# Six tiles of their own for the transposed probabilities, scale products four at a time, and new engine orders

## The chip, the core and the metric

The kernel runs on one core of a Trainium2 chip. The core has five engines that each work through their own list of instructions in order: TensorE (PE, matrix products), VectorE (DVE), ScalarE (ACT), GpSimd (POOL) and SyncE (SP), which in this kernel issues the DMA transfers. The metric is the time of one execution on the device in microseconds, as the median of several runs.

## What is computed

Attention over pooled queries, then a bilinear feed-forward layer. The inputs `q`, `k`, `v` are 4 batches x 8 heads x 1152 positions x 64.

```python
def _attn_ref(q, k, v):
    B, H, S, D = q.shape
    factor = 2
    scale = 1.0 / np.sqrt(D)
    q_pool = q.reshape(B, H, S // factor, factor, D).mean(axis=3)
    scores = scale * np.matmul(q_pool, k.transpose(0, 1, 3, 2))
    scores = scores - np.max(scores, axis=-1, keepdims=True)
    attn = np.exp(scores)
    attn = attn / (np.sum(attn, axis=-1, keepdims=True) + 1e-09)
    return np.matmul(attn, v).astype(np.float32)

def _moe_ref(x, w_a, w_b, w_out):
    a = x @ w_a
    b = x @ w_b
    return (a * b @ w_out).astype(np.float32)
```

`x` is the attention's output with the heads side by side: 2304 tokens x 512. `w_a` and `w_b` are 512 x 1536, `w_out` is 1536 x 512.

## The kernel before, in words

**Staging.** Work on a batch goes by pairs of heads, in passes: a pass takes some query rows of one pair, in blocks of 128 rows of one head. Batch 0 has eight passes, two rounds over its four pairs. For each block PE makes the scores (L682, from batch 2 on L685 with operands split into two f16 parts), DVE copies them with a bound on the row's maximum (L717, `sm_max`), ACT takes the exponential (L724), and DVE makes the factor of the row from its sum (L728, L734). What follows depends on the pass:
- In the first four passes (`N_PE = 4`) PE transposes the f32 block in pieces of up to 4 x 128 columns into PSUM (L760, `tr_pe`), ACT or DVE copies each piece into the tile `pt` (L771 or L773, `tr_out`, by the letters of `EVICT`), and PE multiplies it by `v` (L804, `pv_f`). The row factors go through a diagonal matrix (L776, `r_diag`; L780, `r_wide`; L784, `r_mul`).
- In all later passes ACT and DVE write the scaled block as two f16 parts, high and low, into one of three buffers `p` (L737, L741), SP issues one DMA transpose of it into `pt` (L747, `transpose`), and PE multiplies by the two f16 parts of `v` (L838, `pv`).

ACT moves the product out of PSUM (L848, `x_copy`), and ACT, POOL and DVE split and scale it into the f16 parts `xt` (L871, L875, L881). Beside the first four passes run the weights, 12 slices f of 128 columns: loaded by SP (L552), rebuilt from 64-bit numbers by ACT, POOL and DVE (L558, L577, L581, L588), their magnitude taken on ACT or DVE (L567, L570) and summed over the partitions on PE (L597, `w_sum`). DVE makes a scale of each sum (L600, `w_scale`; L605), and ACT and DVE or POOL split each slice into two parts (L622; L626, L631, L635). Then comes the feed-forward layer by tiles of 256 tokens: PE multiplies `xt` by the weights of `a` and `b` (L919, `moe_mm`, 24 products for each f of a tile), ACT and DVE form `g` from them with the scales in `cc` (L926, L931), ACT and POOL split `g` (L936, L939), and PE multiplies by `w_out` (L945).

**The tile of transposed probabilities.** `pt` is one tile in SBUF, `[128, 2, NCH, NR * 128]` in f16: two parts, nine chunks of 128 positions, and `NR = 6` slots of 128 columns. Each block has the slot of its number modulo 6. The early passes see the same bytes as f32, in the view `ptf`, and use two slots' columns of it for two heads. Waits between instructions that touch one tile are drawn by the framework from the regions that they touch.

**Scales.** `w_cc` (L609) multiplies the two scales of one f by the scale of batch 0 into `cc`, two instructions of one element in each partition; it is called once for each of the 12 f. For batches 1 to 3 one instruction does all f at once (L519).

**What sets the order.** Everything above is a task of the class `Plan`: an engine, a duration, a key, a function and the names that it reads and writes. The five rows of the table `ORDERS` (PE, DVE, ACT, POOL, SP) list the numbers of the tasks in the order in which each engine gets them. `Plan.order` merges the five into one program order; the instructions of one engine then run strictly in that order.

Of the kernel before, what the change touches and what calls it, by code (L numbers as in the profile page):

```python
# [7 lines left out]
F32 = mybir.dt.float32  # L8
# [20 lines left out]
REMN = 64  # L29
N_PE, EVICT = 4, "ADADA"  # L30
# [180 lines left out]
    ),  # L211
)

# [964 lines left out]
```

## Time and profile before

| | |
|---|---|
| median of 3 runs | 839.35 us (837.95 to 842.45) |
| profiled execution | 840.88 us, span in the trace 839.1 us |
| mean granted clock of TensorE | 0.981 of full speed |
| PE busy | 781.5 us (93%) |
| DVE busy | 619.8 us (74%) |
| ACT busy | 580.0 us (69%) |
| POOL busy | 242.4 us (29%) |
| instructions in the trace | 21333 |

The profile records one execution. The span runs from the first instruction to the last; the execution's own time is 1.8 us longer. An engine is busy while it carries out an instruction, not while it waits for a semaphore. Where the profile names a releaser for an idle time, it is the instruction or transfer whose end came last before the idle engine went on.

### The profile page before, as it was taken

The numbers are of one execution on the slowest core, as the hardware profiler recorded it, in microseconds if no ns is written. First come the engines' busy times: TensorE is split into PE (matmuls) and PEld (weight loads), VectorE is DVE, ScalarE is ACT, GpSimd is POOL, SyncE is SP. The second block draws the span as 40 slices with busy tenths as digits, with TensorE's granted clock in tenths as the row PEclk, the third lists the DMA queues.
The fourth block names the chain that finished last, engine by engine and source line by source line (L and its number), as shares of the span: only waits on it lengthen the run. The fifth ranks groups of instructions, "written<-read, shape, count | busy, mean of one in ns | idle before, by whom it ended". The sixth has DMA issues, their size and how long they took to land.

```text
span 839.1 us, 21333 instructions
## 1 busy us (share of the span) xinstructions
PE 781.5 (93%) x8864; PEld 603.4 (72%) x8864; DVE 619.8 (74%) x1215; ACT 580.0 (69%) x986; POOL 242.4 (29%) x226
## 2 busy tenths in 40 slices
PE   6877458989999998999999999999999999999998
PEld 3654336767677776787777877887788788887886
DVE  4998878978998898999999999889687634032110
ACT  4999897878778787788888789777666643233222
POOL 5668674323310222201132104101301221301203
PEclk9998969999999999999999999999999999999999
DMA  7655748899999999999999999899867616000100
GB/s 262 208 188 204 208 144 192 211 199 196 209 212 210 195 200 189 232 173 217 192 185 211 182 206 194 164 171 173 151 127 127 127 30 128 13 26 1 27 2 25
DMA packets 316289, 132.32 MB, mean 158 GB/s; under 512 B 300832, under 2 KB 302880, under 8 KB 316192
## 3 DMA queue, kind: packets, MB, share of 16 engines
q1 hardware_dynamic: 316192, 130.96, 75.1%
q8 instruction: 69, 1.13, 0.5%
q14 instruction: 28, 0.23, 0.1%
HBM read 50.72 MB, written 4.72 MB: 66 GB/s over the span
## 4 chain that ended last, share of the span: by engine, by line
PE 57%; DVE 2%; DMA 1%; ACT 0%; issue 0%
PE ab L919 26%; PE ab L945 15%; PE sps L685 8%; PE xps L838 8%; DMA pt<-p 1%; DVE p L741 1%; DVE s L717 1%; PE sps L682 0%; DVE g L931 0%; ACT g L926 0%; DVE o L951 0%; PE xps L496 0%; ACT p L737 0%; ACT s L724 0%; PE xps L429 0%
## 5 line engine op out<-in xcount | busy, mean ns | idle before, releaser
L919 PEld LDWEIGHTS <-wab 128*128 128x128 f16 x2592 | 252.2, 99 | 37.3 <-issue 6.3
L919 PE MATMUL ab<-xt,wab 128*128 128x256 f16 x2304 | 262.7, 274 | 2.7 <-DVE xt L881 0.9
L724 ACT ACTIVATE s<-s,st 128x1152 f32<-128x1152 f32 x144 | 179.9, 1250 | 34.5 <-DVE s L717 34.0
L939 POOL TENSOR_TENSOR gl<-g,gh 128x256 fp32r<-128x256 f32 x108 | 94.5, 880 | 358.1 <-ACT gh L936 349.7
L741 DVE SCALAR_TENSOR_TENSOR p<-s,st,p 128x1152 f16<-128x1152 f32 x128 | 181.5, 1424 | 10.0 <-ACT p L737 9.5
L737 ACT ACTIVATE p<-s,st 128x1152 f16<-128x1152 f32 x128 | 159.0, 1248 | 37.9 <-DMA pt<-p 13.3
L945 PE MATMUL ab<-wo,gh 128*128 128x512 f32 x432 | 139.8, 405 | 1.7 <-DVE g L931 1.7
L682 PE MATMUL sps<-k,q 64*128 64x512 f32 (+3 forms) x448 | 103.9, 557 | 22.6 <-DVE s L717 10.5
L926 ACT ACTIVATE g<-ab,cc 128x256 f32<-128x256 f32 (+1 forms) x144 | 55.4, 415 | 90.4 <-PE ab L919 90.3
L717 DVE TENSOR_SCALAR_CACHE_REDUCE s<-sps 128x1152 f32<-128x1152 f32 x72 | 96.7, 1350 | 25.7 <-PE sps L682 24.5
L717 DVE TENSOR_SCALAR_CACHE_REDUCE s<-sps,ksc 128x1152 f32<-128x1152 f32 x72 | 101.0, 1410 | 15.7 <-PE sps L685 15.3
L838 PE MATMUL xps<-pt,vs 128*64 128x128 f16 (+1 forms) x3888 | 109.3, 215 | 1.4 <-DMA pt<-p 1.1
L838 PEld LDWEIGHTS <-vs 128*64 128x64 f16 x3888 | 100.5, 110 | 13.5 <-issue 11.6
L931 DVE SCALAR_TENSOR_TENSOR g<-ab,cc,g 128x256 f32<-128x256 f32 (+1 forms) x144 | 55.2, 410 | 72.6 <-ACT g L926 72.6
L682 PEld LDWEIGHTS sps<-k,q 64*128 64x128 f32 (+1 forms) x448 | 48.5, 187 | 75.4 <-issue 52.4
L945 PEld LDWEIGHTS ab<-wo,gh 128*128 128x128 f32 x432 | 77.9, 188 | 20.4 <-ACT g L926 1.7
L945 PE MATMUL ab<-wo,gl 128*128 128x512 f32 x216 | 85.4, 395 | 0.0
L936 ACT ACTIVATE gh<-g 128x256 fp32r<-128x256 f32 x108 | 43.8, 411 | 54.8 <-PE ab L945 54.1
L685 PE MATMUL sps<-k,q 64*128 64x512 f16 (+3 forms) x624 | 65.5, 341 | 0.0
L685 PEld LDWEIGHTS <-q 64*128 64x128 f16 (+1 forms) x720 | 36.2, 97 | 39.6 <-issue 7.0
L581 POOL TENSOR_SCALAR xt<-xt 128x512 f16<-128x512 f32 x22 | 51.9, 2357 | 35.3 <-ACT xt L577 25.9
L419 POOL TENSOR_TENSOR q<-qraw 128x576 f32<-128x576 f32 (+2 forms) x20 | 25.0, 1250 | 92.3 <-PE sps L682 48.9
(120 smaller groups left out, 737.1 us busy)
## 6 DMA issues: line engine op xcount, KB each, us to landing
k<-in_k_dram SPq DMA_DIRECT2D x19, 576.0 KB, 4.7
vraw<-in_v_dram SPq DMA_DIRECT2D x17, 576.0 KB, 4.9
xt<-in_w_ab_dram SPq DMA_DIRECT2D x15, 512.0 KB, 3.6
qraw<-in_q_dram SPq DMA_DIRECT2D x12, 576.0 KB, 4.5
out_dram<-o SPq DMA_DIRECT2D x16, 256.0 KB, 3.8
xt<-in_w_out_dram SPq DMA_DIRECT2D x7, 512.0 KB, 3.3
g<-in_w_ab_dram SPq DMA_DIRECT2D x5, 512.0 KB, 4.2
wab<-in_w_ab_dram SPq DMA_DIRECT2D x4, 512.0 KB, 3.5
```

Of the source, the lines that this page charges most:

```text
L682: nc.tensor.matmul(out, q, k, start=True, stop=True)
L685: nc.tensor.matmul(out, q[:, hq], k[:, hk], start=(hq, hk) == (0, 0), stop=(hq, hk) == (1, 0))
L717: nc.vector.tensor_scalar(out=s_t[sbuf(i)], in0=sps[:, at:at + S], scalar1=-1.0 / 16.0 if u is None else ksc[:, u, 4:5], scalar2=None, op0 ...
L724: nc.scalar.activation(out=s, in_=s, func=AF.Exp, scale=-1.0, bias=t[:, 0:1], accum_out=t[:, 1:2])
L737: nc.scalar.activation(out=p_t[pbuf(i)][:, 0], in_=s_t[sbuf(i)], func=AF.Copy, scale=st_t[i % NST][:, 3:4])
L741: nc.vector.scalar_tensor_tensor(out=p[:, 1], in0=s, scalar=st_t[i % NST][:, 3:4], in1=p[:, 0], op0=ALU.mult, op1=ALU.subtract)
L838: nc.tensor.matmul(xps[half(e), at:at + w], vs[:, c, e, hv], pt[:, hp, c, c0:c0 + w], start=(c == 0 and n == 0), stop=(c == NCH - 1 and n ...
L919: nc.tensor.matmul(dst if t < 8 else dst.rearrange("p (b n) -> p b n", b=B), wab[:, f, 1 - m, a, c], moe_x(t, b, c), start=(n == 0), stop= ...
L926: nc.scalar.activation(out=g_t[:, f, c], in_=ab[j][:, 1, c], func=AF.Copy, scale=cc[:, b, f, 0:1])
L931: nc.vector.scalar_tensor_tensor(out=g, in0=ab[j][:, 0, c], scalar=cc[:, b, f, 1:2], in1=g, op0=ALU.mult, op1=ALU.mult)
L939: nc.gpsimd.tensor_tensor(out=gl_t[j], in0=g_t[:, f], in1=gh_t[j].bitcast(F32), op=ALU.subtract)
L945: nc.tensor.matmul(acc[u], g[:, us], wo[:, f, a], start=(first and n == 0), stop=(last and n == 2))
```

## The change

`pt` becomes a list of six tiles, one for each slot, each `[128, 2, NCH, 128]`; `ptf` becomes a list of f32 views of them. In the early passes a head's block now lies in the tile of its own slot. `w_cc` makes the scales of four f (`CC_F = 4`) in one instruction with eight elements in each partition: three instructions in place of 24. Since this changes the number of tasks and their numbering, every row of `ORDERS` is new, and the order is another one. In DVE's order before, L609 stands 12 times ahead of the first L881 that frees an L919 product; in the new order it stands there twice. Before, nine of PE's sums L597 stand ahead of the first L919, now ten.

```diff
@@ -27,6 +27,7 @@
 P_SCALE = 2.0 ** 14
 
 REMN = 64
+CC_F = 4
 N_PE, EVICT = 4, "ADADA"
 N_WHOLE, TWO_ROUNDS = 2, (0,)
 
@@ -55,159 +56,159 @@
 ORDERS = (
     (
-        12, 18, 24, 26, 38, 28, 7, 30, 32, 44, 34, 35, 54, 56, 151, 58, 52, 60, 62, 157, 64, 65, 163, 177, 82, 167,
...
+        12, 18, 7, 24, 26, 38, 28, 30, 32, 44, 34, 35, 56, 54, 151, 58, 52, 60, 62, 157, 163, 165, 177, 64, 65, 169,
...
@@ -328,7 +329,7 @@
     xt = [T(f"xt{j}", [128, 2, KC, 512], F16) for j in range(2)]
     xr = T("xr", [128, B, 2, KC, REMN], F16)
     x32 = [T("x32", [128, NQ])]
-    pt = T("pt", [128, 2, NCH, NR * 128], F16)
+    pt = [T(f"pt{j}", [128, 2, NCH, 128], F16) for j in range(NR)]
     kn = [T(f"k{j}", [128, S]) for j in range(2)]
     qraw = T("qraw", [128, 2, NQ])
     vraw = T("vraw", [128, NCH, 128])
@@ -391,7 +392,7 @@
     kzf = [x.bitcast(F16).rearrange("p (a n) -> p a n", a=2) for x in kz]
 
     ident, diag = g_t[:, 0, 0:128], [g_t[:, 1 + e, 0:128] for e in range(2)]
-    ptf = pt.rearrange("p a c n -> p (a c n)").bitcast(F32).rearrange("p (a c n) -> p a c n", a=2, c=NCH)
+    ptf = [x.rearrange("p a c n -> p (a c n)").bitcast(F32).rearrange("p (c n) -> p c n", c=NCH) for x in pt]
     vf = [vs.rearrange("p c e h d -> p (c e h d)").bitcast(F32).rearrange("p (c n) -> p c n", c=NCH), vraw]
 
     def vbuf(p):
@@ -604,11 +605,10 @@
     def w_inv(f):
         nc.vector.reciprocal(out=wsc[:, 0, f], in_=wsc[:, 1, f])
 
-    def w_cc(f):
-        for m in range(2):
-            nc.vector.tensor_scalar(
-                out=cc[:, 0, f, m:m + 1], in0=wsc[:, 1, f, m:m + 1], scalar1=vb[:, 0, 0:1], scalar2=None, op0=ALU.mult
-            )
+    def w_cc(f0, f1):
+        nc.vector.tensor_scalar(
+            out=cc[:, 0, f0:f1], in0=wsc[:, 1, f0:f1], scalar1=vb[:, 0, 0:1], scalar2=None, op0=ALU.mult
+        )
 
     def w_dst(f, m, hl):
         return wab[:, f, m, hl] if m < 2 else wo[:, f, hl]
@@ -743,9 +743,8 @@
         )
 
     def transpose(i):
-        c0 = 128 * blocks[i].slot
         nc.sync.dma_start_transpose(
-            out=pt[:, :, :, c0:c0 + 128].rearrange("p a c n -> p (a c) n"),
+            out=pt[blocks[i].slot].rearrange("p a c n -> p (a c) n"),
             in_=p_t[pbuf(i)].rearrange("p a n -> p (a n)"),
         )
 
@@ -763,9 +762,9 @@
         at = 0
         for i in sorted(set(i for i, _ in chunks)):
             cs = [c for x, c in chunks if x == i]
-            m, w = 64 * (blocks[i].slot - blocks[i].head), 128 * len(cs)
+            w = 128 * len(cs)
             src = acc[j][:, at:at + w].rearrange("p (c n) -> p c n", n=128)
-            dst = ptf[:, blocks[i].head, cs[0]:cs[0] + len(cs), m:m + 128]
+            dst = ptf[blocks[i].slot][:, cs[0]:cs[0] + len(cs)]
             at += w
             if on == "A":
                 nc.scalar.activation(out=dst, in_=src, func=AF.Copy)
@@ -798,11 +797,11 @@
                 r=[f"acc{j}"], w=[name])
         return out
 
-    def pv_f(p, at, m):
+    def pv_f(p, at, slots):
         for c in range(NCH):
             for e in range(2):
                 nc.tensor.matmul(
-                    xps[half(e), at:at + 128], vf[p % 2][:, c, 64 * e:64 * e + 64], ptf[:, e, c, m:m + 128],
+                    xps[half(e), at:at + 128], vf[p % 2][:, c, 64 * e:64 * e + 64], ptf[slots[e]][:, c],
                     start=(c == 0), stop=(c == NCH - 1),
                 )
 
@@ -834,11 +833,11 @@
     def pv(runs, at, w):
         for c in range(NCH):
             for n, (hp, hv) in enumerate(((0, 0), (0, 1), (1, 0))):
-                for e, c0 in enumerate(runs):
+                for e, (t, c0) in enumerate(runs):
                     nc.tensor.matmul(
                         xps[half(e), at:at + w],
                         vs[:, c, e, hv],
-                        pt[:, hp, c, c0:c0 + w],
+                        pt[t][:, hp, c, c0:c0 + w],
                         start=(c == 0 and n == 0),
                         stop=(c == NCH - 1 and n == 2),
                     )
@@ -848,7 +847,7 @@
         nc.scalar.activation(out=x32[j][:, x0:x0 + w], in_=xps[:, at:at + w], func=AF.Copy, scale=scale)
 
     def unit(slots, at, w, key):
-        runs = [128 * t for t in slots] if len(slots) > 1 else [128 * slots[0], 128 * slots[0] + w]
+        runs = [(t, 0) for t in slots] if len(slots) > 1 else [(slots[0], 0), (slots[0], w)]
         add("PE", 0.04 + 1.49 * w / 128, key - 9, pv, (runs, at, w), r=[f"pt{t}" for t in slots] + ["vsh", "vsl"],
             w=["xps"], mode=2)
 
@@ -972,8 +971,9 @@
             key = 1000 + 3 * len(steps)
             steps.append((t, f))
             scs = [f"cc{b}{f}" for b in bs]
-            if t == 0:
-                add("DVE", 0.14, -5, w_cc, (f,), r=[f"wsc{f}", "vb0"], w=[f"cc0{f}"])
+            if t == 0 and f % CC_F == 0:
+                of = range(f, f + CC_F)
+                add("DVE", 0.12, -5, w_cc, (f, f + CC_F), r=[f"wsc{x}" for x in of] + ["vb0"], w=[f"cc0{x}" for x in of], port=True)
             r = xs + [f"w{f}{m}{hl}" for m in range(2) for hl in "hl"]
             for m in range(2):
                 add("PE", 1.311, key + m, moe_mm, (t, f, m, j), r=r, w=[f"acc{j}"])
@@ -1093,7 +1093,7 @@
                 prep_vmax(nxt.p, nxt.parts[0] == "even", ps_.end - 4)
             if ps_.pe:
                 parts = moved(ps_, i - 2, r)
-                add("PE", 2.02, i - 10, pv_f, (ps_.p, at, 64 * slots[0]), r=[f"pt{t}" for t in slots] + parts + vbuf(ps_.p),
+                add("PE", 2.02, i - 10, pv_f, (ps_.p, at, tuple(slots)), r=[f"pt{t}" for t in slots] + parts + vbuf(ps_.p),
                     w=["xps"], mode=2)
                 add("PE", 0.3, i - 10, r_wide, (), r=["g1", "g2", "ones"], w=["xps"], mode=2)
                 leaving = [(at, XE + at, 128)]
```

The numbers behind the names in the following rows are those of the tiles; "waits" names the counters for which an instruction waits, DMAHW0 to DMAHW7 being those of DMA transfers. In the new file the lines of the functions stand one lower or higher (L771 is L770, L773 is L772, L747 is L746, L609 stays, L741 stays).

ACT before, at the last evictions of the fourth pass (L771) between a softmax step (L737) and the magnitude of a weight slice (L567):

```order
L724 ACTIVATE s0_75,st_80<-s0_75,st_80 128x1152 [waits DVE_49]
L871 ACTIVATE xt0_63<-x32_66 128x256 [waits DVE_49]
L737 ACTIVATE p2_83<-s2_77,st_80 128x1152 [waits Activation_49]
L771 ACTIVATE pt_67<-ab1_101 128x128 [waits DMAHW2_49]
L771 ACTIVATE pt_67<-ab1_101 128x128
L776 ACTIVATE g_84<-g_84,st_80 128x128
L567 ACTIVATE wab_61,wmx_96<-o1_90 128x512 [waits DVE_49]
L577 ACTIVATE xt1_64<-xt1_64 128x512 [waits DMAHW0_49]
```

ACT now, at the same two evictions (L770):

```order
L737 ACTIVATE p1_87<-s1_81,st_85 128x1152 [waits DVE_49,Activation_49]
L724 ACTIVATE s2_82,st_85<-s2_82,st_85 128x1152 [waits DVE_49]
L847 ACTIVATE x32_66<-xps_107,vsc_99 128x128 [waits PE_49]
L770 ACTIVATE pt2_69<-ab1_106 128x128
L770 ACTIVATE pt3_70<-ab1_106 128x128
L559 ACTIVATE o1_95<-xt1_64 128x512 [waits DVE_49]
L622 ACTIVATE wo_62<-o0_94 128x512
```

The two evictions have moved ahead of the L737 that writes `p2`, and the counter of a DMA is gone from them.

DVE before, at its last copy of a transposed piece (L773), among the weight slices (L626, L588):

```order
L626 SCALAR_TENSOR_TENSOR wab_61<-o1_90,wsc_97,wab_61 128x512 [waits Activation_49]
L626 SCALAR_TENSOR_TENSOR wab_61<-wab_61,wsc_97 128x512 [waits DVE_49,Activation_49]
L588 SCALAR_TENSOR_TENSOR wab_61<-wab_61,xt1_64 128x512 [waits DMAHW5_49,Pool_49]
L626 SCALAR_TENSOR_TENSOR wab_61<-z2_91,wsc_97,wab_61 128x512 [waits Activation_49]
L773 COPY pt_67<-ab0_100 128x4x128 [waits DMAHW1_49]
L881 TENSOR_SCALAR xt0_63<-xt0_63,vsc_94 128x2x256
L588 SCALAR_TENSOR_TENSOR wab_61<-wab_61,xt1_64 128x512 [waits DMAHW7_49,Activation_49,Pool_49]
L784 SCALAR_TENSOR_TENSOR x32_66<-x32_66,xps_102 128x128 [waits Activation_49]
```

DVE now, at the same copy (L772):

```order
L734 RECIPROCAL st_85<-st_85 128x1
L606 RECIPROCAL wsc_102<-wsc_102 128x2 [waits DVE_49]
L741 SCALAR_TENSOR_TENSOR p1_87<-s1_81,st_85,p1_87 128x1152
L772 COPY pt3_70<-ab0_105 128x512
L741 SCALAR_TENSOR_TENSOR p2_88<-s2_82,st_85,p2_88 128x1152 [waits Activation_49]
L717 TENSOR_SCALAR s1_81,st_85<-sps_104 128x1152 [waits DVE_49,PE_49]
L626 SCALAR_TENSOR_TENSOR wab_61<-wab_61,wsc_102 128x512 [waits Activation_49]
```

The copy now stands between the low parts of two blocks of the next pass (L741), ahead of the weight slices that it followed, and waits for nothing on its own.

SP before, from the first DMA transpose on:

```order
L747 DMA_TRANSPOSE pt_67<-p1_82 128x18x128 [waits PE_49]
L552 DMA wab_61<-in_w_out_dram 128x1024 [waits DMAHW6_49,DVE_49]
L411 DMA k0_68<-in_k_dram 128x1152 [waits PE_49]
L552 DMA xt1_64<-in_w_ab_dram 128x1024 [waits DMAHW5_49,DMAHW0_49,DVE_49]
L414 DMA qraw_70<-in_q_dram 128x2x320 [waits DMAHW7_49,Pool_49]
L552 DMA xt1_64<-in_w_out_dram 128x1024 [waits DMAHW1_49,DVE_49,Activation_49]
L552 DMA g_84<-in_w_ab_dram 128x1024
L747 DMA_TRANSPOSE pt_67<-p2_83 128x18x128 [waits PE_49]
L552 DMA xt1_64<-in_w_ab_dram 128x1024 [waits DMAHW2_49,DMAHW5_49,DVE_49,Activation_49]
L552 DMA xt1_64<-in_w_ab_dram 128x1024 [waits DMAHW7_49,DMAHW3_49,DVE_49]
L747 DMA_TRANSPOSE pt_67<-p0_81 128x18x128 [waits DMAHW4_49,PE_49]
```

SP now, from the first DMA transpose on:

```order
L746 DMA_TRANSPOSE pt4_71<-p1_87 128x18x128 [waits DVE_49,PE_49]
L746 DMA_TRANSPOSE pt5_72<-p2_88 128x18x128 [waits DVE_49,PE_49]
L553 DMA g_89<-in_w_ab_dram 128x1024 [waits DMAHW4_49,DMAHW6_49,DVE_49,Pool_49]
L553 DMA xt1_64<-in_w_ab_dram 128x1024 [waits DMAHW5_49,DMAHW0_49,DVE_49]
L553 DMA xt1_64<-in_w_out_dram 128x1024 [waits DMAHW1_49,DVE_49]
L412 DMA k0_73<-in_k_dram 128x1152 [waits DMAHW7_49,PE_49]
L553 DMA wab_61<-in_w_out_dram 128x1024
L746 DMA_TRANSPOSE pt0_67<-p0_86 128x18x128 [waits DVE_49,PE_49]
L553 DMA xt1_64<-in_w_ab_dram 128x1024 [waits DMAHW5_49,DMAHW2_49,DVE_49]
L746 DMA_TRANSPOSE pt1_68<-p1_87 128x18x128 [waits DMAHW3_49,PE_49]
L553 DMA xt1_64<-in_w_ab_dram 128x1024 [waits DMAHW4_49,DMAHW6_49,DVE_49,Activation_49]
```

The first two transposes now follow each other; before, the load of `k`, that of `qraw` and four weight loads stood between them.

## Rows read from the trace of the kernel before

**Rows 1.** Busy time by stretch (first column; then its length)
```profile
core 0: us, PE busy (x) PEld busy (x) DVE busy (x) ACT busy (x) POOL busy (x), PEclk, DMA share, GB/s
...
95.00:135.00 40.00, 20.02 (x138) 13.80 (x135) 29.50 (x58) 28.48 (x53) 24.71 (x13) 0.74 0.57 158
135.00:341.00 206.00, 199.13 (x2472) 146.84 (x2470) 181.56 (x337) 162.72 (x252) 57.13 (x54) 0.99 1.06 206
341.00:600.00 259.00, 258.47 (x3521) 200.98 (x3522) 243.48 (x451) 207.47 (x312) 50.34 (x59) 1.00 1.02 189
...
sum 839.00, PE 781.49 PEld 603.44 DVE 619.77 ACT 580.02 POOL 242.42; mean PE 130.25 PEld 100.57 DVE 103.30 ACT 96.67 POOL 40.40
```

**Rows 2.** Page, part 4: the chain that ended last, by engine
```profile
PE 57%; DVE 2%; DMA 1%; ACT 0%; issue 0%
```

**Rows 3.** Waits from 95 to 135 us: us in total, times, longest
```profile
ACT pt L771 <- DMA pt<-p: 4.1, 1, 4.1
...
DVE pt L773 <- DMA pt<-p: 3.6, 1, 3.6
```

**Rows 4.** Timeline of ACT: start, us, instruction, [idle before <-releaser]
```profile
97.32 1.28 ACT L737 ACTIVATE p<-s,st 128x1152 f16<-128x1152 f32 x1
102.69 0.45 ACT L771 ACTIVATE pt<-ab 128x128 f32<-128x128 f32 x2 [4.09 <-DMA pt<-p]
```

**Rows 5.** Timeline of SP's queue, 95 to 135 us
```profile
97.12 3.89 SPq L747 DMA_TRANSPOSE pt<-p  x1
...
120.53 3.41 SPq L747 DMA_TRANSPOSE pt<-p  x1
...
131.32 5.18 SPq L747 DMA_TRANSPOSE pt<-p  x2
```

**Rows 6.** Timeline of PE, from 95 us to the end of batch 0
```profile
106.46 0.59 PE L597 MATMUL xps<-wmx,one 128*128 128x2 f32 x2 [7.42 <-ACT wab L567]
...
117.05 3.44 PE L804 MATMUL xps<-pt,vraw 128*64 128x128 f32 x36 [0.96 <-DVE wsc L600]
...
127.59 3.72 PE L804 MATMUL xps<-pt,vraw 128*64 128x128 f32 x36 [4.38 <-DVE x L784]
...
132.00 1.16 PE L919 MATMUL ab<-xt,wab 128*128 128x256 f16 x9
...
179.10 0.27 PE L682 MATMUL sps<-k,q 64*128 64x128 f32 x1 [2.11 <-issue]
...
190.58 2.79 PE L919 MATMUL ab<-xt,wab 128*128 128x256 f16 x24
...
328.12 1.67 PE L838 MATMUL xps<-pt,vs 128*64 128x128 f16 x53 [0.85 <-DMA pt<-p]
...
335.49 2.20 PE L682 MATMUL sps<-k,q 64*128 64x512 f32 x10 [1.39 <-DVE s L717]
```

**Rows 7.** Timeline of DVE, 95 to 172 us
```profile
108.17 0.32 DVE L609 TENSOR_SCALAR cc<-wsc,vb 128x1 f32<-128x1 f32 x2
...
125.14 0.69 DVE L773 COPY pt<-ab 128x512 f32<-128x512 f32 x1 [3.57 <-DMA pt<-p]
...
132.13 0.29 DVE L784 SCALAR_TENSOR_TENSOR x<-x,xps 128x128 f32<-128x128 f32 x1 [1.81 <-ACT x L848]
...
133.66 0.35 DVE L881 TENSOR_SCALAR xt<-xt,vsc 128x512 f16<-128x512 f16 x1 [1.17 <-POOL xt L875]
...
171.97 0.74 DVE L626 SCALAR_TENSOR_TENSOR wab<-o,wsc,wab 128x512 f16<-128x512 f32 x1
```

**Rows 8.** Instructions on the tile `cc`: duration ns min/median/max
```profile
L609 DVE TENSOR_SCALAR cc<-wsc,vb x24: 193/200/205, 89.7 to 171.8; 128x1 f32<-128x1 f32 x24
L519 DVE TENSOR_SCALAR cc<-wsc,vb x3: 219/229/233, 325.0 to 634.6; 128x24 f32<-128x24 f32 x3
```

**Rows 9.** The tile `pt`: its transposes, and one who waited for it
```profile
L747 SPq DMA_TRANSPOSE pt<-p x128: 2389/2880/6917, 97.1 to 710.3; - x128
...
  ACT p L737: 13.3, 10
```

288 rows, old and new, of the table ORDERS are left out of this document.

## Prediction

> **What bounds the kernel now.** I read the busy times by stretch first, since a share over the whole span hides that the limits change [rows 1]. TensorE (PE) is busy for 781.5 of 839.0 us in all. From 135 to 600 us it works 457.6 of 465 us (199.13 + 258.47) at a granted clock of 0.99 to 1.00: there PE is the bound, and the end of the kernel moves with the moment at which PE's steady stream of L919 products begins, as long as nothing new starves it. The chain of waits agrees: PE is 57% of it, no other engine over 2% [rows 2]. From 95 to 135 us it is otherwise: PE 20.0, VectorE (DVE) 29.5 and ScalarE (ACT) 28.5 us busy of 40, at a granted clock of 0.74 on average (so part of it at 1.2 and not 2.4 GHz). All three stand idle for 10 to 20 us in the same stretch, so this is where a change can pay.
>
> What stops them is in the list of waits of this stretch. Two entries are odd: the eviction of a transposed block into `pt` waits for a DMA that writes `pt`, on ACT for 4.1 us and on DVE for 3.6 us [rows 3]. The last pass that transposes on PE and the first that transpose by DMA overlap here, in different slots of the one tile `pt`; the data asks for neither wait. The timelines give the sequence:
> - ACT ends L737 at 98.6 us (97.32 + 1.28) and stands until 102.69, for the transpose that SP issued at 97.12 [rows 4, 5]. Behind the blocked eviction, in order, stands the weight maximum of L567; PE's sum over it (L597) starts at 106.46 after 7.42 us idle [rows 6]. That is a shadow of the one 4.09 us stall, not a further term.
> - DVE stands from 121.57 to 125.14 for the transpose issued at 120.53 [rows 5, 7]. That one was itself late: SP issued it just when PE's product L804 of 117.05 had ended (117.05 + 3.44). The next transposes left at 131.32, when the L804 of 127.59 had ended [rows 5, 6]. So `pt` was handed to and fro between a product and a transpose that have no slot in common.
> - Behind DVE's late copy come L804 on PE (4.38 us idle before it) and then DVE's L784 and L881 (1.81 and 1.17 us); the first L919 product starts at 132.00 [rows 6, 7].
>
> **The change part by part**, against the profiled execution's own 840.88 us (1.53 above the median of 839.35).
>
> 1. *Six tiles in place of one.* No eviction and no transpose has the other's slot any more, so both false waits go. In the new order the last two evictions on ACT follow each other with no DMA in their waits, and the last copy on DVE has no wait at all. ACT's stall: **-4.09**. DVE's stall: **-3.57**. I add them up, since they lie 19 us apart and on two engines that both work on the softmax and the weights ahead of the first L919.
> 2. *The hand-over at the end of this stretch.* The new table puts the last copy on DVE ahead of the final L741, so the last L804 needs no longer wait for it; what is left is the hand-over from PE to ACT, POOL and DVE. At best DVE's 1.81 and 1.17 go (2.98), at worst nothing does. I take the middle: **-1.5**.
> 3. *Scale products, four f at a time.* 24 instructions of 200 ns become 3 [rows 8]. Two in a row take 0.32 us [rows 7], so the second adds 0.12. Ahead of the L881 that frees the first L919 products stand 12 of them before, and 2 of the new ones now. Those are 128x8; their nearest row is the 128x24 product of L519, 0.23 us [rows 8]. 12 x 0.12 less 2 x 0.23 is **-1.0**. The other 12 lie after 135 us, where PE is the bound and DVE has 24.4 of 206 us free [rows 1]: nothing. The cost of grouping is that f waits for the scale of f+3; the sums and scales of f 0 to 7 stand ahead of the first L919 in both orders, so it is covered there. Without that cover `g` would be late and PE would stand for an `ab` buffer.
> 4. *Evictions and transposes into contiguous tiles.* The copies read and write as many elements: nothing. The 128 DMA transposes have a median of 2.88 us on SP's queue [rows 9]. Bounds for them are the shortest that the trace has, 2.39 us, and 2.88; PE's one row that waits for a transpose shows 0.85 us [rows 6], so the sum takes 2.88, no change.
>    The Trainium skill, DMA: Bandwidth & Descriptors (Latency and other measured facts), gives a DMA transpose 261 GB/s with a non-contiguous middle dimension and some 350 to 400 when contiguous; no row here has the contiguous form. By that page the transposes would shorten by a quarter to a third, an estimate, and the result would be the third rival's.
> 5. *The new order elsewhere.* Every engine's table is new, so the waits after 135 us are new as well. Their nearest rows are PE's present ones: 2.11 us at 179.10, 0.85 at 328.12, 1.39 at 335.49 [rows 6], 4.35 in all. At best they vanish (-4.35), at worst they double (+4.35), and an earlier start of PE meets work that is not ready. As PE has been moved forward against engines that were matched to its old pace, I take a value nearer to the doubling, **+2.0**. On SP two transposes now leave back to back, followed by three weight loads and the load of `k`; before, it was one transpose, one load, then `k`.
>
> Sum: 840.88 - 4.09 - 3.57 - 1.5 - 1.0 + 2.0 = 832.7, less the 1.53 between this execution and the median: **831.2**, told as 831.
>
> **Rivals.**
> - *The gain is given back* (839). PE gets to L919 some eight microseconds earlier and stands about as long later, at pass boundaries like the three of part 5. Against it: DVE is free for 24.4 us from 135 to 341 and for 15.5 us from 341 to 600 [rows 1], enough to win 8 back. For it: DVE is busy for 94% of the second of these. 20%.
>   The Trainium skill, Perfetto Trace Analysis (Identifying the Most-Contended Engine), says to work on the engine of highest occupancy; over the span that is PE, from which this change takes nothing, and by that rule alone the time would stay at 839. The stretch from 95 to 135 us disagrees: PE is busy there for 20 of 40 us.
> - *Slower: SP's queue* (845). SP works in order, and a transpose holds it until its block's L741 is done and then for 2.88 us. In the new order the first four transposes stand ahead of weight loads that two of them followed. If the third and fourth leave no earlier than now, at 131.32 [rows 5], the last loads move from 124.11 to some 134, by 10 us; the last L626, now at 171.97 [rows 7], would end near 183. PE has 24 products for each f and begins those of the last at 190.58 now [rows 6], and 8 us earlier, at 182.6, if the rest of the forecast holds: the cover is then just used up. From there each transpose for which SP stands costs PE its length, 3.41 us by the row of 120.53; four of them make 13.6, and 831 becomes 845. Against it: with no false wait the third and fourth should leave earlier. 9%.
> - *More: the transposes get shorter too* (827). The DMA engines are at 1.06 of their time from 135 to 341 us [rows 1], ACT's L737 waits for transposes 13.3 us in ten places [rows 9], and one of PE's three later waits is for one. A transpose shorter by 0.5 to 1 us would take most of the 4.35 of part 5: about 4 us more. 10%.
> - *It does not do what it says* (839): a slot is still shared, or a wait is still drawn. Against it: the new order's rows name six tiles and no such wait. 3%.
>
> **How the numbers follow.** My forecast (831) has 58%, the rivals 20, 9, 10 and 3. A measurement of this kernel tells about 0.5% from no change, 4.2 us: faster means under 835.2. That is nearly all of the forecast (54 of 58), all of the third rival, and a part of the first (6): 70%. Slower is the SP rival: 9%. The rest, 21%, is within. The range takes the sum's ends: all of part 2 and vanishing waits lead to 823, doubled waits with nothing from part 2 to 835; up to 839.5 it takes in two thirds of the cases in which the gain is given back. Outside are some 3% below and 16% above.
>
> **What would show it.** Right: in the profile after, no eviction into `pt` waits for a transpose; between 95 and 135 us DVE and ACT are idle for 4 to 7 us each and not 10 to 12; the first product of `ab` from `xt` starts at 122 to 126 us and not 132.0; PE's busy time stays within some 5 us of 781.5, since the work is the same, and its idle time falls from 57.5 to about 50; DVE has 21 instructions fewer. Wrong in part 5 if the first L919 is early and PE's idle time after 135 us grows by as much. Wrong in the SP rival's way if POOL's and ACT's weight steps wait for loads between 110 and 180 us and PE stands ahead of the last f. The transposes' median tells the third rival: well under 2.88 us if it is so.

## The result, and the profile after

The changed kernel takes 830.56 us (median of 4 runs, 829.7 to 830.76) beside 839.65 us of the kernel before on the same chip: 0.9886 of it, 95% interval 0.9858 to 0.9914. In two later groups of runs the ratio was 0.9859 [0.983, 0.9887] and 0.9851 [0.9823, 0.9879]. By the medians it is faster by 9 to 12 us; the forecast was 831, within 823 to 839.5. The profiled execution took 830.57 us, its span is 828.8 us.

First the busy time by stretch, as in [rows 1]:

```profile
95.00:135.00 40.00, 27.95 (x200) 18.55 (x200) 39.35 (x73) 37.70 (x68) 29.52 (x16) 0.79 0.82 209
135.00:341.00 206.00, 203.67 (x2638) 151.43 (x2636) 187.27 (x341) 167.94 (x256) 55.98 (x57) 1.00 1.07 208
341.00:600.00 259.00, 254.37 (x3408) 197.70 (x3407) 242.15 (x437) 205.06 (x308) 55.39 (x60) 1.00 1.04 187
...
sum 828.80, PE 781.68 PEld 604.14 DVE 623.21 ACT 581.29 POOL 245.44; mean PE 130.28 PEld 100.69 DVE 103.87 ACT 96.88 POOL 40.91
```

The work is the same (PE 781.7 us busy, before 781.5), its idle time fell from 57.5 to 47.1 us. Of these 10.4 us, 7.9 went between 95 and 135 us. DVE, idle there for 10.5 us before, is idle for 0.65 now, and ACT for 2.3 in place of 11.5; I had expected 4 to 7 us for each. Up to the first L918 product at 124 us DVE has next to no idle time left:

```profile
95.00:124.00 29.00, 16.95 (x125) 10.41 (x126) 28.85 (x57) 26.83 (x51) 20.73 (x12) 0.76 0.81 208
```

With 28.85 of 29.00 us busy, DVE is the engine that sets the pace of this stretch now.

Then the timeline of ACT, at the two evictions of [rows 4]:

```profile
94.02 0.39 ACT L847 ACTIVATE x<-xps,vsc 128x128 f32<-128x128 f32 x1
94.27 0.47 ACT L770 ACTIVATE pt<-ab 128x128 f32<-128x128 f32 x2
94.59 0.71 ACT L559 ACTIVATE o<-xt 128x512 f32<-128x512 f32 x1
```

of DVE, at the last copy and the hand-over of [rows 7]:

```profile
97.35 1.60 DVE L741 SCALAR_TENSOR_TENSOR p<-s,st,p 128x1152 f16<-128x1152 f32 x1
98.88 0.68 DVE L772 COPY pt<-ab 128x512 f32<-128x512 f32 x1
99.48 1.80 DVE L741 SCALAR_TENSOR_TENSOR p<-s,st,p 128x1152 f16<-128x1152 f32 x1
...
122.87 0.27 DVE L783 SCALAR_TENSOR_TENSOR x<-x,xps 128x128 f32<-128x128 f32 x1
...
124.37 0.35 DVE L880 TENSOR_SCALAR xt<-xt,vsc 128x512 f16<-128x512 f16 x1 [0.37 <-POOL xt L874]
```

and of PE, at the places of [rows 6]:

```profile
112.46 2.19 PE L803 MATMUL xps<-pt,vraw 128*64 128x128 f32 x36 [0.95 <-DVE wsc L601]
...
119.18 2.19 PE L803 MATMUL xps<-pt,vraw 128*64 128x128 f32 x36 [1.04 <-DVE x L783]
...
123.99 7.08 PE L918 MATMUL ab<-xt,wab 128*128 128x256 f16 x48
```

No eviction has idle time ahead of it. The last copy comes 26 us earlier than before (98.88, not 125.14). The hand-over wait of L783 (L784 before, 1.81 us) is gone, that of L880 (L881 before) is 0.37 and not 1.17 us. The last two L803 products wait 1 us each, and each takes 2.19 us, where those of [rows 6] took 3.44 and 3.72. The first L918 product (L919 before) starts at 123.99, 8.0 us earlier. Two waits of PE close behind the first nine products are gone as well; the kernel before had

```profile
134.06 3.11 PE L919 MATMUL ab<-xt,wab 128*128 128x256 f16 x27 [0.90 <-DVE xt L881]
138.02 0.38 PE L597 MATMUL xps<-wmx,one 128*128 128x2 f32 x2 [0.85 <-ACT wab L567]
```

How much comes before that product, and how much behind it, is read from the busy times of two stretches cut there, of the kernel before (at 132) and of the changed one (at 124):

```profile
132.00:839.10 707.10, 692.27 (x8219) 542.94 (x8218) 515.37 (x986) 472.23 (x776) 156.93 (x176) 1.00 0.79 150
```

```profile
124.00:828.80 704.80, 691.63 (x8217) 543.84 (x8216) 518.48 (x973) 473.85 (x773) 162.13 (x177) 1.00 0.79 150
```

So the 10.3 us of the two spans are 8.0 up to the first product and 2.3 behind it. Two later profiles of the changed kernel have the first product at 123.02 and 123.06, 9.0 us earlier than before.

### The profile page after: what moved, and what is told of

Read it like the earlier page. It is cut to its first block, busy times and chain, and to the rows that moved or that the text cites. A ratio compares the mean times of both kernels' runs of the same rounds, so it can differ in the third digit from the quotient of the medians.

```text
span 828.8 us, 21323 instructions
## 1 busy us (share of the span) xinstructions
PE 781.7 (94%) x8864; PEld 604.1 (73%) x8864; DVE 623.2 (75%) x1194; ACT 581.3 (70%) x986; POOL 245.4 (30%) x226
## 5 line engine op out<-in xcount | busy, mean ns | idle before, releaser
L918 PEld LDWEIGHTS <-wab 128*128 128x128 f16 x2592 | 252.4, 98 | 31.7 <-issue 1.1
L918 PE MATMUL ab<-xt,wab 128*128 128x256 f16 x2304 | 262.1, 274 | 0.2 <-DVE g L930 0.2
L741 DVE SCALAR_TENSOR_TENSOR p<-s,st,p 128x1152 f16<-128x1152 f32 x128 | 183.8, 1439 | 15.0 <-ACT p L737 14.1
L737 ACT ACTIVATE p<-s,st 128x1152 f16<-128x1152 f32 x128 | 159.3, 1251 | 44.3 <-DMA pt<-p 23.4
L682 PE MATMUL sps<-k,q 64*128 64x512 f32 (+3 forms) x448 | 103.3, 556 | 15.2 <-DVE s L717 7.0
L682 PEld LDWEIGHTS sps<-k,q 64*128 64x128 f32 (+1 forms) x448 | 48.2, 187 | 69.3 <-issue 49.4
L944 PEld LDWEIGHTS ab<-wo,gl 128*128 128x128 f32 x216 | 40.6, 188 | 11.0 <-POOL gl L938 1.3
```

What stands on the lines that cost most here:

```text
L682: nc.tensor.matmul(out, q, k, start=True, stop=True)
L737: nc.scalar.activation(out=p_t[pbuf(i)][:, 0], in_=s_t[sbuf(i)], func=AF.Copy, scale=st_t[i % NST][:, 3:4])
L741: nc.vector.scalar_tensor_tensor(out=p[:, 1], in0=s, scalar=st_t[i % NST][:, 3:4], in1=p[:, 0], op0=ALU.mult, op1=ALU.subtract)
L918: nc.tensor.matmul(dst if t < 8 else dst.rearrange("p (b n) -> p b n", b=B), wab[:, f, 1 - m, a, c], moe_x(t, b, c), start=(n == 0), stop= ...
L944: nc.tensor.matmul(acc[u], g[:, us], wo[:, f, a], start=(first and n == 0), stop=(last and n == 2))
```

## The experiments

My theory was that the false waits on the one tile make the gain. The rivals: the new order makes it; the grouped scales do; the contiguous transposes do. Each of the first four runs does or undoes one part.

**Six tiles alone, in the order of before.** The edit of `pt`, `ptf` and their users stands as in the diff; `ORDERS` and `w_cc` are those of before.

> The kernel before with its own order and its 24 scale products, and nothing but the six tiles. Theory A (the false waits on the one tile are the gain): ACT's 4.09 us and DVE's 3.57 us go, the first L919 product comes at 124 to 125 us in place of 132.0, and the time falls by 6 to 9 us, to 831 to 834. Theory B (the new order is the gain): the old order brings the next late thing in their place, the first L919 comes at 130 us or later, and the time stays at 837 to 840. Theory D (contiguous tiles shorten the transposes): their median falls from 2.88 to 2.4 us or less.

Measured: 831.28 us, 0.9897 [0.9867, 0.9928] of the kernel before (840.67 in this group). A second series for a comparison with the changed kernel on the same chip:

> The six tiles in the old order with 24 scale products, once more. If my parts 3 and 5 are worth what I put on them (-1.0 and +2.0), this kernel is faster than the changed one by about 1 us. If the new order wins something of its own beside the tiles (PE starts on L918 at 124.0 in place of 126.3 us), this kernel is slower by 1 to 3 us: 831.5 to 833.

Measured: 831.3 us, 0.9889 [0.986, 0.9918], just below the second branch. The timelines of ACT and PE in this second execution:

```profile
99.98 1.24 ACT L737 ACTIVATE p<-s,st 128x1152 f16<-128x1152 f32 x1
101.13 0.43 ACT L770 ACTIVATE pt<-ab 128x128 f32<-128x128 f32 x2
```

```profile
116.14 3.81 PE L803 MATMUL xps<-pt,vraw 128*64 128x128 f32 x36 [0.96 <-DVE wsc L600]
122.82 2.19 PE L803 MATMUL xps<-pt,vraw 128*64 128x128 f32 x36 [0.47 <-DVE x L783]
125.57 1.16 PE L918 MATMUL ab<-xt,wab 128*128 128x256 f16 x9
```

Theory A holds: the tiles alone make the kernel faster by 9 to 10 us. The eviction follows L737 at once, and the wait of 4.38 us ahead of the last L803 is 0.47. The first L918 product, though, came at 125.6 here and at 126.3 in the first series, not at 124 to 125. The reason lies ahead of the change: L737 started at 99.98 (101.14 in the first series) and at 97.32 before. From the start of L737 to the first product it is 34.7 us before (132.00 - 97.32), and 25.6 and 25.2 with six tiles: 9.1 to 9.5 us are gone, more than the 7.66 of the two stalls.

**The new order with the one tile.** The changed kernel, its grouped scales included, with `pt`, `ptf` and their users as before.

> The changed kernel, new order and grouped scales, but with the one tile of before. The program's waits show what is left of the false ones in this order: the first transpose waits for DVE's last copy, and the fourth for the last product of the last early pass and not for the one before; no eviction waits for a transpose. Theory A in its strict form (without the six tiles the stalls come back): 837 to 840. Theory B (the order alone avoids them, since it puts the evictions ahead of the transposes): the first transpose leaves 0.5 to 1 us later than at 99.05, the fourth 1 to 2 us later than at 120.18, and the time is 830.5 to 833.

Measured: 829.64 us, 0.9891 [0.9862, 0.9919]. Its SP queue and PE:

```profile
98.33 5.65 SPq L747 DMA_TRANSPOSE pt<-p  x2
...
122.06 2.69 SPq L747 DMA_TRANSPOSE pt<-p  x1
```

```profile
118.82 3.29 PE L804 MATMUL xps<-pt,vraw 128*64 128x128 f32 x36 [1.98 <-DMA pt<-p]
124.33 5.42 PE L919 MATMUL ab<-xt,wab 128*128 128x256 f16 x48
```

Theory B holds as well. The new order, with the grouped scales, has the whole gain as far as the medians tell, although two false waits are left: the last L804 stands 1.98 us for a transpose, and the fourth transpose leaves at 122.06 (with six tiles at 120.18). In this order the evictions are through before the first transpose is issued, so there is nothing for them to wait for. Tiles and order are two cures of one ill, and their gains don't add up: 9 to 10 us by the tiles, 11 by the order, 9 to 12 by both.

The six tiles do count in the new order, though, up to the first product. DVE's last copy into `pt` starts in this run at

```profile
97.57 0.68 DVE L773 COPY pt<-ab 128x512 f32<-128x512 f32 x1
```

and the first product follows 26.8 us later (124.33 - 97.57). With six tiles it is 25.1 us (123.99 - 98.88, and the same in the two other profiles of the changed kernel). So the one tile, with the false waits that are left, costs 1.6 us there. At the end of the kernel the medians cannot show so little: the changed kernel's own three are 830.56, 829.59 and 828.12 us, in other groups of runs than this one.

**The scales one by one.** The changed kernel with this in `w_cc`:

```diff
-        nc.vector.tensor_scalar(
-            out=cc[:, 0, f0:f1], in0=wsc[:, 1, f0:f1], scalar1=vb[:, 0, 0:1], scalar2=None, op0=ALU.mult
-        )
+        for f in range(f0, f1):
+            for m in range(2):
+                nc.vector.tensor_scalar(
+                    out=cc[:, 0, f, m:m + 1], in0=wsc[:, 1, f, m:m + 1], scalar1=vb[:, 0, 0:1], scalar2=None, op0=ALU.mult
+                )
```

> The changed kernel with each of its three grouped scale products as eight instructions of one element, at the same places. My sum: 16 instructions at 0.12 us less two at 0.22 lie ahead of the first L918 product, 1.5 us on DVE; if they are on the path, that product comes at 125 to 125.5 in place of 123.99 and the time is 831.5 to 832. Rival: DVE has slack there (the scale's place lies ahead of the last hand-over, which waits for PE and ACT), the first L918 product moves by less than 0.3 us and the time stays at 830.3 to 830.9.

Measured: 830.47 us, 0.989 [0.987, 0.991]. DVE's timeline has the two groups, and PE's the first product:

```profile
106.23 1.05 DVE L611 TENSOR_SCALAR cc<-wsc,vb 128x1 f32<-128x1 f32 x8
...
112.34 1.05 DVE L611 TENSOR_SCALAR cc<-wsc,vb 128x1 f32<-128x1 f32 x8
```

```profile
124.53 5.41 PE L920 MATMUL ab<-xt,wab 128*128 128x256 f16 x48
```

Eight take 1.05 us where the grouped one took 0.22 and 0.55, so DVE does lose 1.3 us. The first product is 0.5 us later than the 123.99 above, which lies between the two branches; but the whole stretch lies earlier in this execution, and two more profiles of the changed kernel itself, below, have it at 123.02 and 123.06. What the scales cost is seen from DVE's last copy into `pt` on:

```profile
97.97 0.68 DVE L774 COPY pt<-ab 128x512 f32<-128x512 f32 x1
...
123.41 0.28 DVE L785 SCALAR_TENSOR_TENSOR x<-x,xps 128x128 f32<-128x128 f32 x1
```

From there to L785 (L783 in the changed kernel), for which PE's sum L598 waits just ahead of the first product, it takes 25.4 us, and to the first product 26.6. In the three profiles of the changed kernel it is 24.0 and 25.1. The 1.3 us that DVE loses arrive in full at the first product, which fits a DVE that has no idle time there. Most of them are still there some 15 us later, at the next sum L598, which starts 42.1 us behind the copy here and 40.8 there:

```profile
140.05 0.28 PE L598 MATMUL xps<-wmx,one 128*128 128x2 f32 x2
```

```profile
139.69 0.28 PE L598 MATMUL xps<-wmx,one 128*128 128x2 f32 x2
```

Whether they are there at the end of the kernel, these runs don't tell. The median is not above the first one of the changed kernel, but it is 0.9 and 2.4 us above the two later ones, and the changed kernel did not run in this group.

**One tile with the slot outermost, old order.**

```diff
-    pt = [T(f"pt{j}", [128, 2, NCH, 128], F16) for j in range(NR)]
+    pt_all = T("pt", [128, NR, 2, NCH, 128], F16)
+    pt = [pt_all[:, j] for j in range(NR)]
```

> As the six tiles in the old order, but the six slots are slices of one tile that has the slot as its outermost index, so that each slot's bytes lie together. If what counts is that a slot's region can be told apart from the others: the same time as with six tiles, within 1 us. If each tile has to be one for itself for the waits to go: the time of the kernel before, 839 to 840.

Measured: 832.96 us, 0.9912 [0.989, 0.9934], with no idle time ahead of an eviction; from L737 to the first product it takes 25.2 us (99.60 to 124.79), as with six tiles. The median is 1.7 us above that of six tiles in the same group (831.28), more than the 1 us I had allowed, but the runs of the two overlap (830.74 to 834.12, 828.36 to 835.0). What counts is not how many tiles there are but that a slot's bytes lie together.

**One false wait at a time, old order.** One slot gets a tile of its own, the five others stay columns of one tile (slot 4 alone in the first run, slot 5 alone in the second). Each slot's f32 view uses its own columns only:

```diff
+    ptx = T("pt", [128, 2, NCH, (NR - 1) * 128], F16)
+    pty = T("pty", [128, 2, NCH, 128], F16)
+    pt = [pty if t == OWN else ptx[:, :, :, 128 * at_x(t):128 * at_x(t) + 128] for t in range(NR)]
...
+    ptf = [py if t == OWN else px[:, :, :, 64 * at_x(t):64 * at_x(t) + 64] for t in range(NR)]
```

> The kernel before in its own order, where slot 4 alone has a tile of its own and the other five slots stay columns of one tile. By the program's waits ACT's eviction then waits for no transpose, while DVE's last copy still waits for the transpose into slot 5, and that one for the product of slots 0 and 1. Theory A with terms that add up (ACT's stall 4.1, DVE's 3.6 and more behind it): ACT's stall is gone, DVE's stays at 3 to 4 us, the time is 834.5 to 836.5. Rival 1 (the two stalls are alternatives, either gone is enough): 830 to 832. Rival 2 (only both together count): 838 to 841.

> The same with slot 5 alone in a tile of its own: ACT's eviction still waits for the transpose into slot 4, DVE's last copy for none. Theory A with terms that add up: ACT's stall stays at 4.1 us, DVE's is gone, the time is 834.5 to 836.5. Rival 1 (either gone is enough): 830 to 832. Rival 2 (only both together count): 838 to 841.

Measured: 836.02 us, 0.9947 [0.9924, 0.9971], and 835.52 us, 0.9953 [0.9924, 0.9981], beside 840.4. The waits between 95 and 135 us, first where DVE's side is shared, then where ACT's is:

```profile
DVE pt L778 <- DMA pt<-p: 4.0, 1, 4.0
```

```profile
ACT pt L776 <- DMA pt<-p: 4.1, 1, 4.1
```

Each run keeps the stall that was left to it and loses the other; each has about half of the gain (4.4 and 4.9 us), and the halves make the whole (9.4 to 9.8 us with six tiles). By the medians the terms add up. Their sizes are seen from the start of L737 to the first product: 129.97 - 99.04 = 30.9 us without ACT's stall, 127.16 - 98.03 = 29.1 without DVE's, 34.7 before. ACT's stall is worth 3.8 us, near its 4.09, and DVE's 5.6, more than its 3.57. The difference lies behind the copy: without DVE's stall the last product of the fourth pass takes 2.19 us, with it 3.67. First the run where DVE's stall is left, then the one where it is gone:

```profile
125.73 3.67 PE L809 MATMUL xps<-pt,vraw 128*64 128x128 f32 x36 [4.37 <-DVE x L789]
129.97 1.16 PE L924 MATMUL ab<-xt,wab 128*128 128x256 f16 x9
```

```profile
124.41 2.19 PE L809 MATMUL xps<-pt,vraw 128*64 128x128 f32 x36 [0.49 <-DVE x L789]
127.16 1.16 PE L924 MATMUL ab<-xt,wab 128*128 128x256 f16 x9
```

**Does a later first product cost as much at the end?** The changed kernel, with copies on ACT ahead of the last `x_copy` of the fourth pass (12, then 24):

```diff
...
+        if p == 3 and at == 128:
+            for _ in range(12):
+                nc.scalar.activation(out=junk, in_=junk, func=AF.Copy)
```

> The changed kernel with twelve idle copies of 128x128 on ACT ahead of the last copy of x of the fourth pass, about 3.6 us that nothing uses, so that the first L918 product comes about 2.5 to 3.6 us later than 123.99. Theory: from there on PE is the bound, nothing absorbs the delay, the time is 833 to 834.5. Rival (the steady part has slack, other engines set the end): 830.3 to 831.5, with PE's idle time after the first L918 product shorter by as much.

> The changed kernel once more, for the two others of this group to be compared with it on the same chip: 829.5 to 831.5.

> The delay of the run with twelve idle copies doubled to 24, about 8 us of ACT. Theory (PE is the bound from the first L918 product on, nothing absorbs): that product comes 5 to 7 us later than 123.99 and the time is as much longer, 835.5 to 837.5. Rival (later slack gives it back): below 833.

Measured: with 12 copies 832.0 us, between the two branches, the first product at 125.49, less late than expected; the step is too small to tell anything. With 24, beside the changed kernel on the same chip: 836.66 against 829.59 us, and the first products

```profile
129.84 6.86 PE L924 MATMUL ab<-xt,wab 128*128 128x256 f16 x48
```

```profile
123.02 7.08 PE L918 MATMUL ab<-xt,wab 128*128 128x256 f16 x48
```

6.8 us later at the start; at the end 7.1 us later by the medians, 6.1 by the two profiled executions (834.9 and 828.8 us of span). Of a delay of the first product little or nothing is given back. The second kernel of this group is the changed one; against it, six tiles in the old order took 1.7 us more (831.3). That agrees with the branch in which the new order wins a little of its own, but the runs overlap (827.61 to 831.07, 830.62 to 834.97).

**A slow start of PE's stream.** The 48 products at 123.99 took 7.08 us, those of the two runs above with the same order 5.41 and 5.42. An attempt to have that always, in `r_wide` of the fourth pass's second half:

```diff
...
+            for n in range(6):
+                nc.tensor.transpose(acc[1][:, 0:128], ident, ident)
```

> The changed kernel with six transposes of 128x128 on PE that nobody reads, in its idle time between the row factors of the fourth pass (L779) and the sum L598, 1.7 us before the first L918 product. In the changed kernel's profiles the first 48 of these products took 7.08 us, in those of two kernels with the same order 5.41. Theory (the granted clock at the start depends on PE's work just before): with the extra work they take 5.4 to 5.9 us and the time falls by 1 to 1.7 us, to 828 to 829. Rival (it is the phase of the clock and not this gap): 6.5 us or more and no change in time.

> The changed kernel a third time, for the one above to be compared with: 829.5 to 830.6, its first 48 L918 products in 7.0 to 7.1 us if the slow start is the kernel's own, in 5.4 in some executions if it is chance.

Measured: 827.35 us, 0.9847 [0.9822, 0.9872], beside 828.12 us of the changed kernel, which itself came out lower than I had expected. PE's timeline with the extra work, then without:

```profile
120.53 0.87 PE L785 MATMUL ab<-g 128*128 128x128 f32 x6
...
123.00 5.41 PE L924 MATMUL ab<-xt,wab 128*128 128x256 f16 x48
...
137.21 1.47 PE L924 MATMUL ab<-xt,wab 128*128 128x256 f16 x12 [1.32 <-DVE st L728]
138.52 0.28 PE L598 MATMUL xps<-wmx,one 128*128 128x2 f32 x2
```

```profile
123.06 7.08 PE L918 MATMUL ab<-xt,wab 128*128 128x256 f16 x48
...
138.76 0.28 PE L598 MATMUL xps<-wmx,one 128*128 128x2 f32 x2
```

The theory holds for the products: 5.41 us. It does not for the time. PE then stands 1.32 us for DVE, and the sum L598 behind it starts at 138.52 in place of 138.76: of 1.67 us, 0.24 is left. The 0.8 us between the medians lies within the spread of the runs (825.61 to 829.01 and 824.94 to 829.51).

## Why the prediction was right, step by step

- **Part 1, the false waits: right, and shown.** The two stalls are there, each can be taken away alone, and the terms add up (4.4 and 4.9 us, 9.4 to 9.8 together). What I did not see is that the new order takes both stalls away even with the old tile. In the changed kernel the gain of 9 to 12 us cannot be shared out between the six tiles and the order; what the tiles add in the new order is 1.6 us up to the first product.
- **Part 2, the hand-over (-1.5): near in size, wrong in place.** The shadow of DVE's stall is about 2 us (5.6 in place of 3.57), of which 1.5 is the last product of the fourth pass, 2.19 us in place of 3.67. I had named the hand-over from ACT and POOL to DVE's L784 and L881. These start behind the first product (132.13 and 133.66 us, against 132.00), and what PE loses to them is the 0.90 us ahead of its tenth product. All six profiles of the old order have that wait, with six tiles too (there L880 still waits 1.18 us); no profile of the new order has it.
- **Part 3, grouped scales (-1.0): right up to the first product, open at the end.** DVE saves 1.3 us, it is never idle there, and the first product comes 1.4 us later, counted from the last copy, when the scales are made one by one. In the times (830.47 us beside 828.12 to 830.56) an effect of 1 us can neither be seen nor ruled out.
- **Part 4, contiguous tiles: right that nothing comes of it.** In the old order the transposes have a median of 3.12 and 3.09 us with six tiles, 3.05 with the slot outermost, 3.08 and 3.13 with five slots still interleaved, and 2.88 in the kernel before. In the new order it is 3.14 to 3.19 in the three profiles of the changed kernel and 3.17 with the one interleaved tile. In neither order is the contiguous form clearly the shorter one, and the third rival is out. The Trainium skill, DMA: Bandwidth & Descriptors (Latency and other measured facts), gives a higher rate for the contiguous case, and it ties the loss to the M2S half of a transfer, which the page's Terms call the read side. What became contiguous here is the written side. Taken for that side, as the prediction took them, the page's figures would give 1.9 to 2.2 us, an estimate; the measured medians show none of it. Why 2.88 became 3.1 is open; two runs that keep five slots interleaved have it too, so it is not the contiguous form.
- **Part 5, the new order (+2.0): most likely wrong in sign.** From the first product to the end it takes 707.1 us before; in the profiles of six kernels with the old order (that one, both series of six tiles, the slot outermost, and the two with one slot apart) 704.2 to 707.5, 706.2 on average. In the eight of the new order (three of the changed kernel, the one tile, the scales one by one, the 12 and the 24 copies, the extra transposes) it is 702.8 to 706.8, 704.5 on average. So the order gained about 1.7 us there where I had it lose 2.0; with one execution of each kernel and ranges that overlap, the size is uncertain. Of the three waits that I had counted, the 2.11 us ahead of L682 at 179.10 and the 1.39 at 335.49 are gone from the changed kernel, and the one for a transpose stays (0.98 us at 336.90). The 0.90 and 0.85 us close behind the first products are gone too; I had not counted them.
- **The sum.** Forecast -8.2. Up to the first product the changed kernel gains 8.0 to 9.0 us in its three profiles, where parts 1 to 3 have 10.2; behind it the order gains about 1.7, where part 5 has a loss of 2.0. Together that is about -10 to -11, and the medians show -9 to -12. The mechanism was right; that the first median came within 0.5 us of the forecast is partly luck, since the errors go to opposite sides and the two later groups show 11.5 and 11.9 us.
- **Rivals.** The gain is not given back: a delay of 6.8 us that was put in cost 6.1 to 7.1 at the end. SP's queue did not become the bound: the third transpose left at 114.67 and the fourth at 120.18, not at 131.32, and PE works 203.67 of the 206 us from 135 to 341 us. And no eviction waits for a transpose, so the change does what it says.

Open: the start of the kernel up to L737 took 0.7 to 3.8 us longer in the five profiles of old-order kernels with another layout than in the one of before. Between 40 and 70 us the granted clock was 0.84 to 0.89 in them and 0.94 before. The one interleaved tile in the new order has 0.86, so it does not take the new layout. What makes it, these runs don't tell.

## What to carry to other kernels

A wait for a transfer that moves data the waiting instruction never touches is a sign that two regions can't be told apart: lay the index that separates them outermost (in one tile or several), or order the program so that the one kind is through before the other starts; either was enough here, and doing both did not pay twice. Ahead of the moment at which the bound engine's steady stream begins, a microsecond counts nearly in full: a delay of 6.8 us cost 6.1 to 7.1. Which engine's microseconds they are has to be read again after each change: once the false waits were gone, DVE was busy for 28.85 of the 29 us ahead of that moment, and 1.3 us more work on it moved the moment by 1.4.

## What the runs showed that I had not expected

- With one interleaved tile, slots that share no column still drew waits where one side wrote them through an f32 view (4.0 and 4.1 us in the two runs with one slot apart, whose f32 views kept to their slot's columns). With the slot outermost in the same single tile they drew none.
- The same 48 products took 7.08 or 5.41 us. The granted clock of these 7 us (124 to 131) was 0.76 in the changed kernel and 1.00 with the scales one by one. PE had been idle for 1.70 and 1.51 us ahead of the sum L598; with six transposes put into that gap (0.89 us of idle time left) it was 5.41. The three profiles of the changed kernel all had 7.08, so it belongs to the kernel's own timing. It costs the changed kernel little: the two runs without six tiles or without grouped scales go through these products in 5.42 and 5.41 us, and then PE stands 1.23 and 1.32 us for DVE, as it does with the six transposes.
